# Three changes of order in an attention and mixture-of-experts kernel: loads ahead of DRAM moves, a product ahead of a turn, a routing round half a unit later

## The chip, the cores and the metric

The kernel runs on one core of a Trainium2 chip. A core has five engines that run side by side, each with its own queue of instructions: TensorE (PE in the profile, its weight loads PEld), VectorE (DVE), ScalarE (ACT), GpSimd (POOL) and SyncE (SP), which here only issues transfers (DMAs). The metric is the device time of one execution in microseconds (us), as the median of several runs.

## The reference

```python
def _attn_ref(q, k, v, S1, S2):            # q, k, v: 4 x 4 x 1088 x 32, S1, S2: 8 x 32
    def phi(x):
        a = np.einsum('rd,bhsd->bhsr', S1, x)
        b = np.einsum('rd,bhsd->bhsr', S2, x)
        return np.einsum('bhsi,bhsj->bhsij', a, b).reshape(*x.shape[:-1], r * r)
    q_p, k_p = phi(q), phi(k)
    kv = np.einsum('bhsf,bhsd->bhfd', k_p, v)
    z = np.sum(k_p, axis=2)
    num = np.einsum('bhsf,bhfd->bhsd', q_p, kv)
    den = np.einsum('bhsf,bhf->bhs', q_p, z)[..., None] + 1e-06
    return num / den

def _moe_ref(x, w_gate, w1, w2):           # x: 4352 x 128, 8 experts, w1: 128 x 1024, w2: 1024 x 128
    logits = x @ w_gate
    P = np.exp(logits - logits.max())
    for _ in range(8):
        P /= P.sum(1, keepdims=True) + 1e-09
        P /= P.sum(0, keepdims=True) + 1e-09
        P *= N / E
    for e in range(E):
        out += P[:, e:e + 1] * (np.maximum(x @ w1[e], 0.0) @ w2[e])
```

The output of the attention, with its heads side by side, is the x of the experts. Everything is float32.

## The kernel before

Attention runs batch by batch. For a batch, `keys_sums` multiplies the keys' features into the values, `times(b, c)` multiplies the two repeated halves of the queries' features for one third c of the batch in place (`ph`, times `rb`; L550 on DVE), `tops(b, c)` multiplies these features with the keys' sums on PE (L559, L563), and `over(b, c)` divides (L572 the reciprocal, L574 the quotient, L578 a turn, all on DVE). Batch b also prepares its successors: `transpose_q` turns the loaded queries of a later batch (L387 on DVE, 128x1088), and `queries_ab` projects them (L523 on PE) and sends the results through DRAM (`qa`, `qb`). All products that ACT or DVE read from PSUM, in attention and in the experts' first layer alike, take turns in four banks, `bank()`.

The experts are eight two-layer networks over 4352 rows. The rows are worked on in groups. The first groups, of experts 0 to 2, need no routing weights: they fill PE while attention and routing run. A unit of this work is a step with four matmuls of the first layer (L1183), their evacuation with the ReLU on ACT (L1187, out to `hb`), and products of the second layer (L1643). Seven products of block sums do the work of eight there; the sums of a block's activations are three instructions on DVE (L1204, one double and two single). When all seven are summed, ACT copies the four banks of sums out (L990 to L1007) and DVE adds these up at its leisure (L981, L984).

Attention and routing are generators. Each `yield` hands over a number of units, and `fill` (L1753) puts so many steps of the experts' work between the instructions before and behind the yield. `fill` also counts the steps in `passed`, and `aside` holds work that is due when a count is reached. The order on PE, DVE and ACT is the order of this program; each engine goes through its own in turn.

The later groups, of experts 1 to 7, are weighted, and their first layer needs combinations ("forms") of the blocks of W1. `forms_ahead` makes them, expert by expert, in nine pieces that `forms_at` hangs into `aside`. The first piece, `loads`, issues five transfers on SP's queue: two moves from W1 to the DRAM array `wl` (`raw_of_first`, L284) and three loads of W1's blocks into places of SBUF that attention has left (`area`; by `copied`, L304): `kx`, `ph`, `v`, `kp` and `rb`. Next, ACT turns signs (`turn`, L307), POOL issues transfers that add another block to what was turned (`plus`, L297), and SP issues transfers that write the results to `wl` and `wf` (L304). Experts 1 and 2 are due in batch 2, 3 to 7 (`forms_of_five`) in routing. The first move of expert 3 also waits for the first logits (`all_there`). The transfers on SP and on POOL are kept in the order of the program.

Routing (from L707) computes logits and then eight rounds. A round sums the rows of the routing matrix (L734), takes the reciprocal (L735), waits 1.25 units, scales (L738), sums the columns of each partition (L741, `cs`), waits 3 units, sums over the partitions by two matmuls with ones (L745, the bank `pc`), takes the reciprocal (L748) and scales (L751). The last round's result is turned (L755) and written to DRAM (`pT`), from where the weighted groups load it.

Of the kernel before, what the change touches and what calls it, by code (L numbers as in the profile page):

```python
# [43 lines left out]
def kernel(  # L44
# [24 lines left out]
    ITERS = 8  # L69
# [206 lines left out]
    def split(t):  # L276

        return t.rearrange("p (k b f) -> p k b f", k=2, b=2)

    def raw_of_first(e):  # L280

        w = fast[e][0]
        for out, x in ((w[upper], moe_w1[e][upper]), (split(w)[lower, :, 0], split(moe_w1[e])[lower, :, 0])):
            ins = tc.keep_in_program_order(nc.sync.dma_start(out=out, in_=x))  # L284
            if all_there:
                tc.add_manual_dep(ins.ins, all_there.pop(), SYNC, reason="behind the last x")

    def forms_ahead(e, area):

        w = split(moe_w1[e])  # L290
        fast[e] = [dram.tile([P, F], F32, name=f"{n}{e}") for n in ("wl", "wf")]
        wl, wf = (split(t) for t in fast[e])
        d, t3, z = (x.rearrange("p (k f) -> p k f", k=2) for x in area)
        t3 = t3[lower]

        def plus(out, x):
            tc.keep_in_program_order(nc.gpsimd.dma_start(out=out, in_=x, accum_op=Alu.add))  # L297

        def copied(queue, out, x):
            if queue in last_moves:  # L300
                with tc.issue_after(last_moves.pop(queue).ins):
                    queue.dma_start(out=out, in_=x)
            else:
                tc.keep_in_program_order(queue.dma_start(out=out, in_=x))  # L304

        def turn(out, x):
            nc.scalar.activation(out=out, in_=x, func=Act.Copy, scale=-1.0)  # L307

        def loads():
            raw_of_first(e)  # L310
            copied(nc.sync, d, w[:, :, 0])
            copied(nc.sync, t3, w[lower, :, 1])
            copied(nc.sync, z[lower], w[upper, :, 1])

        def turn_all():
            turn(area[0], area[0])
            plus(area[0], w[:, :, 1])

        def turn_low():
            turn(area[1][lower], area[1][lower])  # L320
            plus(t3, w[upper, :, 1])

        def turn_lowest():
            turn(area[2][lower], area[2][lower])

        def turn_across():
            turn(area[2][upper], area[0][lower])

        def keep_low():
            copied(nc.sync, wf[lower, :, 0], d[lower])  # L330

        def last_sum():
            plus(area[0], area[2])

        def keep_two():
            copied(nc.sync, wl[lower, :, 1], t3)
            copied(nc.sync, wf[upper, :, 0], z[upper])

        def keep_rest():
            copied(nc.sync, wf[:, :, 1], d)  # L340

        return loads, turn_all, turn_low, turn_lowest, turn_across, keep_low, last_sum, keep_two, keep_rest
# [42 lines left out]
    def transpose_q(b, lo=0, hi=S):  # L385
        to = kT if b == 1 else qT
        nc.vector.transpose(out=to[:, lo:hi], in_=loaded["q", b].rearrange("p a d -> p (a d)")[:, lo:hi])  # L387
# [55 lines left out]
    def keys_kept(b):  # L443
        pv = sums_of.pop(b)
        for s in range(2):
            sl = slice(64 * s, 64 * (s + 1))
            if b:
                x, y = kvs[b % 2][sl, :, s, :], pv[sl].rearrange("p i c d -> p i (c d)")[:, :, 0:D + 1]
            else:
                x, y = kvz[sl, :, :, s, :], pv[sl].rearrange("p i c d -> p c i d")  # L450
            nc.scalar.copy(x, y)
# [93 lines left out]
    def third(t, c):  # L545
        return t.rearrange("p i (s c n) -> p i s c n", s=2, c=3)[:, :, :, c]

    def times(b, c):
        ph = third(phs[b % 2], c)
        nc.vector.tensor_tensor(ph, ph, third(rb, c), op=Alu.mult)  # L550
# [87 lines left out]
    def attention(b):  # L638


        follows = b + 1 < B
        apart = 1.4 if follows else 1.05
        keys_sums(b)
        times(b, 0)
        yield 3.6 if b == 1 else 2
        keys_kept(b)
        times(b, 1)
        tops(b, 0)
        if b == 1:
            transpose_q(2)  # L650
        yield apart
        times(b, 2)
        over(b, 0)
        tops(b, 1)
        if b == 1:
            queries_ab(2)
            repeat_a(2)
        if follows:
            repeat_b(b + 1)
        yield apart  # L660
        over(b, 1)
        if b + 1 == B:
            take_over(b, 0, 192, nc.gpsimd)
        yield apart
        tops(b, 2)
        if follows:
            transpose_k(b + 1)
        if b + 2 < B:
            load_k(b + 2)
            load_v(b + 2)  # L670
        yield apart
        over(b, 2)
        if b + 1 < B:
            take_over(b, 0, W9, nc.gpsimd)
            if b + 2 == B:
                forms_of_two()
        else:
            take_over(b, 192, W9, nc.sync)
        if follows:
            yield 0.7  # L680
            keys_ab(b + 1)
            yield 0.7
            if b == 1:
                transpose_q(3)
            keys_products(b + 1, 0)
            yield 1.4
            keys_products(b + 1, 1)
            if b == 1:
                queries_ab(3)
                repeat_a(3)  # L690
            yield 1.4
            keys_products(b + 1, 2)
            yield 1.4
# [11 lines left out]
    def routing():  # L705

        forms_of_five()  # L707
        yield 6
        logits(0)
        logits(1)  # L710
        yield 0.5
        logits_turned()
        logits(2)
        yield 0.5
        logits_turned()
        logits_turned()
        lg = lgp[:, :, 0:E]
        mx = sk.tile([P, 1], F32, tag="mx", name="mx")
        nc.vector.tensor_reduce(out=mx, in_=lg, axis=AX.XY, op=Alu.max)
        yield 2.25  # L720
        pm = bank()[:, 0:P]
        for s in range(2):
            nc.tensor.matmul(pm[64 * s:64 * (s + 1)], mx.to_broadcast([P, 64]), ident, start=True, stop=True,
                             tile_position=(0, 64 * s))
        nc.vector.reduce_max(mx, pm, axis=AX.X)
        nc.vector.tensor_scalar(mx, mx, -1.0, 64 * math.log(2.0), op0=Alu.mult, op1=Alu.add)
        pw = p2s[0]
        nc.scalar.activation(out=pw[:, :, 0:E], in_=lg, func=Act.Exp, bias=mx[:, 0:1])

        step = 1.5 * 2.0 ** (23 - 149 + 64)  # L730
        nc.vector.tensor_scalar(pw[:, :, 0:E], pw[:, :, 0:E], step, step, op0=Alu.add, op1=Alu.subtract)
        for it in range(ITERS):
            rs = sk.tile([P, SA], F32, tag="rs", name="rs")
            nc.vector.reduce_sum(rs, pw, axis=AX.X)  # L734
            nc.vector.reciprocal(rs, rs)  # L735
            yield 1.25
            p1 = p1s[it % 2]
            nc.vector.scalar_tensor_tensor(p1[:, 0:SA], rs.unsqueeze(2).to_broadcast([P, SA, E]), UP,  # L738
                                           pw[:, :, 0:E], op0=Alu.mult, op1=Alu.mult)
            cs = sk.tile([P, E], F32, tag="cs", name="cs")  # L740
            nc.vector.reduce_sum(cs, p1.rearrange("p g e -> p e g"), axis=AX.X)  # L741
            yield 3
            pc = bank()[:, 0:E]
            for s in range(2):
                nc.tensor.matmul(pc[64 * s:64 * (s + 1)], ones[:, 0:64], cs, start=True, stop=True,  # L745
                                 tile_position=(0, 64 * s))
            cr = sk.tile([P, E], F32, tag="cr", name="cr")
            nc.vector.reciprocal(cr, pc)  # L748
            last = it == ITERS - 1
            pw = lgp if last else p2s[(it + 1) % 2]  # L750
            nc.vector.scalar_tensor_tensor(pw[:, :, 0:E], cr.unsqueeze(1).to_broadcast([P, SA, E]),  # L751
                                           float(N) / E * (1.0 if last else UP), p1[:, 0:SA],
                                           op0=Alu.mult, op1=Alu.mult)

        nc.vector.transpose(out=lgT.rearrange("p a s -> p (a s)"), in_=lgp.rearrange("p a e -> p (a e)"))  # L755
        for b in (1, 0, 2, 3):
            tc.keep_in_program_order((nc.gpsimd if b != 1 else nc.sync).dma_start(
                out=pT[:, b * S:(b + 1) * S], in_=lgT[32 * b:32 * b + E].rearrange("p a s -> p (a s)")))
# [1106 lines left out]
```

## Time and profile before

| | |
|---|---|
| time, median of 3 runs | 879.25 us |
| lowest, highest run | 878.93, 882.19 us |
| the profiled execution: its own time | 879.82 us |
| its span, first to last instruction | 878.0 us |
| granted TensorE clock, mean | 1.000 |
| matmuls | 11846, mean times 376 to 517 ns in the experts |
| transfers | 174.64 MB, mean 199 GB/s |

The time of an engine is the sum of its instructions; weight loads (PEld) run beside matmuls. Matmuls overlap: one may start before the one ahead has ended, and their ends are modelled, so the distance from one start to the next is the better measure of PE. A row of the timeline shows the start, the time, the engine, the line, what is written and read, how many instructions of one kind are merged, and in brackets the idle time before them and what ended it. One matmul instruction of the program is two in the profile. A trailing q stands for the engine's sequencer; a row of SPq is the issue of a transfer, not its run. A row of the list of transfers ends with the time from issue to landing.

### The profile page before, as it was taken

To read this page: it belongs to the slowest core of one execution; us is meant where nothing else is said; L and a number is where in the kernel's file an instruction comes from. 1 tells how busy PE (TensorE), PEld (TensorE's weight loads), DVE (VectorE), ACT (ScalarE), POOL (GpSimd) and SP (SyncE) were. 2 spreads that over 40 slices of the span, in tenths; PEclk is the share of its full clock that TensorE was granted. 3 is DMA by queue.
4 is the path that set the end of the run, shared out by engine and by line. 5 is a ranking of instruction groups with operands and counts; after the bars stand their busy time and mean duration, and the time that the engine had idled before them with its cause. 6 is when DMAs were issued, how large, how long until landed. Compare 5 with 4: busy or idle time off the path is not lost.

```text
span 878.0 us, 28825 instructions
## 1 busy us (share of the span) xinstructions
PE 871.7 (99%) x11846; PEld 638.4 (73%) x11846; DVE 790.2 (90%) x1631; ACT 570.4 (65%) x1309; POOL 176.8 (20%) x246
## 2 busy tenths in 40 slices
PE   9999999999999999999999999999999999999998
PEld 6687544566778888887878787878787777766665
DVE  8679688889999999999999999999998999998975
ACT  3455678668676767676666666766766666765653
POOL 2221332121122212221132112221221122200000
PEclk9999999999999999999999999999999999999999
DMA  9998699576778787777786776687577776774430
GB/s 256 284 286 298 135 249 221 136 171 208 219 208 238 214 257 210 199 211 210 209 210 188 210 207 181 184 244 215 159 179 229 217 209 184 204 206 97 119 81 13
DMA packets 97459, 174.64 MB, mean 199 GB/s; under 512 B 29088, under 2 KB 68848, under 8 KB 92480
## 3 DMA queue, kind: packets, MB, share of 16 engines
q1 hardware_dynamic: 74904, 139.65, 50.0%
q0 software_dynamic: 21264, 33.00, 21.9%
q8 instruction: 93, 1.52, 0.7%
q10 hardware_dynamic: 1160, 0.15, 0.1%
q14 instruction: 38, 0.31, 0.1%
HBM read 125.67 MB, written 25.08 MB: 172 GB/s over the span
## 4 chain that ended last, share of the span: by engine, by line
PE 95%; DVE 3%; DMA 1%; issue 0%; DVEq 0%
PE s L1643 42%; PE a L1351 38%; PE a L1183 12%; DMA qx<-in_q_dram 1%; PE a L436 1%; DVE hb L1204 1%; PE a L559 1%; PE a L404 0%; PE s L465 0%; PE a L523 0%; DMA raw<-in_S_dram 0%; PE a L600 0%; PE a L485 0%; PE s L485 0%; DVE rs L734 0%
## 5 line engine op out<-in xcount | busy, mean ns | idle before, releaser
L1351 PE MATMUL a<-xe,w 64*64 64x384 f32 x2164 | 417.3, 483 | 0.0
L1643 PE MATMUL s<-hb,ws 64*64 64x256 f32 (+4 forms) x2980 | 383.2, 383 | 0.0
L1643 PE MATMUL s<-hx,ws 64*64 64x256 f32 (+1 forms) x2908 | 349.4, 376 | 0.0
L1351 PE MATMUL a<-de,w 64*64 64x384 f32 x1600 | 304.6, 483 | 0.0
L1643 PEld LDWEIGHTS s<-hb,ws 64*64 64x64 f32 (+1 forms) x2980 | 205.6, 133 | 65.7 <-issue 17.6
L1643 PEld LDWEIGHTS s<-hx,ws 64*64 64x64 f32 (+1 forms) x2908 | 198.1, 133 | 55.3 <-issue 8.2
L1253 DVE TENSOR_TENSOR hb<-hb 128x512 f32<-128x512 f32 (+1 forms) x340 | 187.8, 577 | 1.3 <-ACT hb L1386 1.1
L1351 PEld LDWEIGHTS a<-xe,w 64*64 64x64 f32 x2164 | 144.5, 133 | 16.3 <-DVE a L1391 1.3
L1386 ACT ACTIVATE hx<-a 128x384 f32<-128x384 f32 x204 | 96.8, 492 | 59.4 <-PE a L1351 57.6
L1386 ACT ACTIVATE hb<-a 128x384 f32<-128x384 f32 x204 | 97.3, 492 | 57.6 <-PE a L1351 56.8
L1183 PE MATMUL a<-xT,w 128*64 128x256 f32 (+3 forms) x576 | 128.2, 453 | 0.0
L1351 PEld LDWEIGHTS a<-de,w 64*64 64x64 f32 x1600 | 110.7, 133 | 19.4 <-ACT hb L1386 0.8
L1253 DVE TENSOR_TENSOR hx<-hx 128x512 f32<-128x512 f32 (+1 forms) x204 | 118.3, 595 | 0.0
L909 POOL DMA_DIRECT2D de<-xe x68 | 57.2, 991 | 299.8 <-PE a L1351 157.9
L1187 ACT ACTIVATE hb<-a 128x256 f32<-128x256 f32 (+3 forms) x150 | 67.7, 453 | 55.3 <-PE a L1183 50.4
L1382 ACT ACTIVATE hb<-a 128x384 f32<-128x384 f32 x136 | 66.7, 491 | 34.1 <-PE a L1351 33.0
L1380 ACT COPY a<-a 128x384 f32<-128x384 f32 x136 | 63.0, 464 | 34.8 <-PE a L1351 34.3
L1391 DVE TENSOR_TENSOR a<-a,hb 128x384 f32<-128x384 f32 x136 | 76.7, 564 | 9.7 <-PE a L1351 8.5
L1183 PEld LDWEIGHTS a<-xT,w 128*64 128x64 f32 x576 | 53.9, 137 | 29.7 <-issue 10.4
L1204 DVE TENSOR_TENSOR hb<-hb 128x416 f32<-128x416 f32 (+7 forms) x90 | 59.8, 664 | 16.2 <-ACT hb L1187 11.2
L1643 PE MATMUL s<-hb,w 128*64 128x256 f32 (+4 forms) x296 | 70.4, 431 | 0.0
L909 POOL DMA_DIRECT2D de<-de x34 | 29.6, 872 | 124.4 <-issue 63.5
(235 smaller groups left out, 1014.2 us busy)
## 6 DMA issues: line engine op xcount, KB each, us to landing
ws<-ws SPq DMA_DIRECT2D x34, 1280.0 KB, 6.5
w<-wl SPq DMA_DIRECT2D x34, 512.0 KB, 7.7
w<-wf SPq DMA_DIRECT2D x33, 512.0 KB, 8.8
px<-pT SPq DMA_DIRECT2D x34, 384.0 KB, 9.5
w<-in_moe_w_dram SPq DMA_DIRECT2D x15, 512.0 KB, 4.7
de<-xe POOLq DMA_DIRECT2D x34, 192.0 KB, 3.3
de<-de POOLq DMA_DIRECT2D x34, 192.0 KB, 8.2
ws<-in_moe_w_dram SPq DMA_DIRECT2D x7, 512.0 KB, 8.3
```

Source lines behind the costliest of these rows:

```text
L436: nc.tensor.matmul(pv[64 * s:64 * (s + 1), i], kp[:, H * t + h].rearrange("p i j -> p (i j)"), vx[:, slots[h], t, :], start=(t == 0 and i ...
L909: tc.keep_in_program_order(nc.gpsimd.dma_start(out=out, in_=x, accum_op=Alu.add))
L1183: nc.tensor.matmul(ph[sl], loaded_w[j][0][:, P * f + H2 * s:P * f + H2 * (s + 1)], sources[j][:, lo:hi], start=True, stop=True, tile_posit ...
L1187: last_relu[:] = [nc.scalar.activation(out=out, in_=ph, func=Act.Relu).ins.name]
L1204: nc.vector.tensor_tensor(out, a, b, op=Alu.subtract)
L1253: nc.vector.tensor_tensor(places(out), places(a), places(b), op=Alu.subtract if off else Alu.add)
L1351: nc.tensor.matmul(out[sl], w[r, c0 + H2 * s:c0 + H2 * (s + 1)], x[r], start=start, stop=stop, tile_position=(H2 * row, H2 * s), skip_grou ...
L1380: witness(k, p, 1, nc.scalar.copy(b, bx))
L1382: witness(k, p, 5, nc.scalar.activation(out=m5s[p], in_=b, func=Act.Copy, scale=1.0 if p else -1.0))
L1386: ins = nc.scalar.activation(out=out, in_=x, func=Act.Relu)
L1391: ins = nc.vector.tensor_tensor(by if what == 1 else raw(k, p, 1, 1), bb[p], m5s[p], op=Alu.add)
L1643: mm = nc.tensor.matmul(sums[g][i][H2 * s:H2 * (s + 1), n * place:n * (place + 1)], w, x, start=c == (2 if halves and row is None else 1) ...
```

## The change

Three orders are changed; no instruction is added or removed.

```diff
@@ forms_ahead @@
         def loads():
-            raw_of_first(e)
+            if e <= 3:
+                raw_of_first(e)
             copied(nc.sync, d, w[:, :, 0])
             copied(nc.sync, t3, w[lower, :, 1])
             copied(nc.sync, z[lower], w[upper, :, 1])
+            if e > 3:
+                raw_of_first(e)
@@ attention @@
         times(b, 1)
         tops(b, 0)
         if b == 1:
+            times(b, 2)
             transpose_q(2)
         yield apart
-        times(b, 2)
+        if b != 1:
+            times(b, 2)
         over(b, 0)
@@ routing @@
             nc.vector.reduce_sum(cs, p1.rearrange("p g e -> p e g"), axis=AX.X)
-            yield 3
+            yield 3.5 if it == ITERS - 2 else 3
             pc = bank()[:, 0:E]
```

For experts 4 to 7 the three loads are issued ahead of the two moves. In batch 1 the third product on `ph` stands ahead of the turn of batch 2's queries, not behind it. In the seventh of the eight rounds of routing, 3.5 units lie between the columns' sums and the matmuls with ones. On PE these matmuls so come one step later: behind two more instructions L1183 and two more L1643. On DVE the two single sums L1204 of a block and one sum L981 come ahead of that round's reciprocal L748, L751, and the next round's L734 and L735. ACT's and POOL's orders stay the same.

## The prediction

> **What bounds the kernel now.** I read the page first: busy time by engine and the chain that ended last.
>
> ```profile
> span 878.0 us, 28825 instructions
> PE 871.7 (99%) x11846; PEld 638.4 (73%) x11846; DVE 790.2 (90%) x1631; ACT 570.4 (65%) x1309; POOL 176.8 (20%) x246
> ...
> PE 95%; DVE 3%; DMA 1%; issue 0%; DVEq 0%
> ```
>
> TensorE (PE) has work for 871.7 of 878.0 us and carries 95% of the chain. A re-ordering can only win what PE loses in gaps, so the next view is the list of PE's waits. Two of its rows name lines that the diff touches.
>
> ```profile
> PE a L745 <- DVE cs L741: 0.4, 1, 0.4
> PE a L523 <- DVE rd L574: 0.3, 1, 0.3
> ```
>
> These figures are too small, because the ends of matmuls are modelled and overlap the next start. The real loss is the distance between two starts less the usual distance, and I read it below from the timelines. The third edit touches no line in this list; there I looked at what ScalarE (ACT) and VectorE (DVE) wait for around the turns of the forms.
>
> **Part by part.** The changed program has the same DMAs and the same arithmetic instructions. Only places in queues move: one DVE product, one pair of PE matmuls with the DVE normalization behind it, and eight moves on SP's queue.
>
> *Batch 1's third ph product (L550) ahead of the turn of batch 2's queries (L387).*
>
> ```profile
> 32.35 1.83 DVE L550 TENSOR_TENSOR ph<-ph,rb 128x768 f32<-128x768 f32 x2 [5.41 <-DMA rb<-qb]
> 35.99 1.31 DVE L387 STREAM_TRANSPOSE qT<-qx 128x1088 f32<-128x1088 f32 x1 [1.82 <-DMA qx<-in_q_dram]
> 37.23 0.92 DVE L550 TENSOR_TENSOR ph<-ph,rb 128x768 f32<-128x768 f32 x1
> ...
> 38.32 0.56 DVE L574 TENSOR_TENSOR rd<-a,rc 128x384 f32<-128x384 f32 x1
> ```
>
> ```profile
> 34.81 0.24 PE L563 MATMUL a<-eps,ones 128*64 128x12 f32 x4
> 34.90 0.69 PE L1183 MATMUL a<-xT,w 128*64 128x288 f32 x4
> ...
> 38.38 0.24 PE L563 MATMUL a<-eps,ones 128*64 128x12 f32 x4
> 38.93 1.20 PE L523 MATMUL a<-qT,wdq 128*64 128x192 f32 x12 [0.31 <-DVE rd L574]
> ```
>
> DVE stands idle for 1.82 us until the queries have landed, turns them, and only then makes the product, whose operands were there all the time. The quotient L574 comes behind it, ends at 38.32 + 0.56 = 38.88, and PE's L523 starts at 38.93. After L563, PE's next start usually follows after 34.90 - 34.81 = 0.09 us; here it took 38.93 - 38.38 = 0.55, so 0.46 us are lost. In the changed order the product (0.92) lies inside the idle 1.82 and ends at about 35.1. The turn still starts at 35.99, and L574 ends 0.92 - 0.08 (the two overlap so much: 35.99 + 1.31 against 37.23) = 0.84 earlier, at 38.04, ahead of the 38.47 at which PE is free. Gain: the whole 0.46 us. If the queries landed before 35.1, the product would delay the turn, but then all of it would also be earlier; I see no loss.
>
> *Experts 4 to 7: arrays ahead of the moves of W1.* The case that shows is expert 5, whose arrays lie in rb.
>
> ```profile
> 118.63 1.82 SPq L284 DMA_DIRECT2D wl<-in_moe_w_dram  x2
> 120.49 2.87 SPq L304 DMA_DIRECT2D rb<-in_moe_w_dram  x3
> ```
>
> ```profile
> wl<-in_moe_w_dram SPq DMA_DIRECT2D x1, 256.0 KB, 6.3
> ...
> rb<-in_moe_w_dram SPq DMA_DIRECT2D x1, 256.0 KB, 7.5
> ```
>
> ```profile
> 125.26 0.52 ACT L1187 ACTIVATE hb<-a 128x416 f32<-128x416 f32 x1 [0.23 <-PE a L1183]
> 128.05 0.63 ACT L307 ACTIVATE rb<-rb 128x512 f32<-128x512 f32 x1 [2.27 <-DMA rb<-in_moe_w_dram]
> ...
> 130.03 0.50 ACT L990 COPY z<-s 64x416 f32<-64x416 f32 x1
> ...
> 134.21 0.52 ACT L1187 ACTIVATE hb<-a 128x416 f32<-128x416 f32 x1
> ```
>
> SP's queue is strictly in order: two moves from DRAM to DRAM, then three loads. The first load was issued at 120.49, landed 7.5 us later at 128.0, and ACT, which had ended at 125.78, held everything behind its turn L307 until 128.05. With the loads first, that load is issued at 118.63. If it takes the landing of the move of equal size it replaces (6.3 us), it is there at 124.9 and the wait is gone; with its own 7.5 us it is there at 126.1 and 0.35 remains. So ACT runs on 1.9 to 2.3 us earlier. The moves come about 2.9 us later, and what they write is read only by the loads of the weighted experts' stage, behind all of routing.
>
> What of it reaches PE? Behind the turn, ACT was late with evacuating PE's banks (L1187), and through it the sums on DVE and then PE:
>
> ```profile
> 134.76 1.03 DVE L1204 TENSOR_TENSOR hb<-hb 128x832 f32<-128x832 f32 x1 [1.45 <-ACT hb L1187]
> ```
>
> ```profile
> 136.36 0.20 PEld L1183 LDWEIGHTS a<-xT,w 128*64 128x64 f32 x4 [0.52 <-ACT hb L1187]
> ...
> 138.53 0.13 PEld L1643 LDWEIGHTS s<-hb,ws 128*64 128x64 f32 x1 [0.58 <-DVE hb L1204]
> ...
> 139.98 0.14 PEld L1643 LDWEIGHTS s<-hb,w 128*64 128x64 f32 x2 [0.21 <-issue]
> 140.76 0.23 PEld L745 LDWEIGHTS a<-cs,ones 128*64 128x64 f32 x4 [0.64 <-ACT hb L1187]
> ```
>
> The weight loads usually stand 0.21 us apart; three gaps of 0.52, 0.58 and 0.64 hold 1.74 - 3 x 0.21 = 1.11 us too much. That is the upper bound of the gain. The lower one is nothing: at 130.03 ACT starts seven copies of finished sums (L990 on), which PE must have finished first, and whatever lead ACT has by then can be lost there. I take 0.4, nearer to nothing, since seven copies at 0.50 fill most of the time from 130.03 to the evacuation at 134.21, whatever ACT's lead was. DVE's late start at 134.76 then moves by about as much.
>
> [...]
>
> *Routing's seventh round half a unit later.* On PE the pair L745 of round seven moves behind one more step (L1183 twice, L1643 twice in the program). On DVE a pair of sums (L1204) and one leisurely sum (L981) move ahead of the reciprocal L748 and the three instructions behind it.
>
> ```profile
> 159.15 0.49 PE L1643 MATMUL s<-hb,w 128*64 128x384 f32 x1
> ...
> 159.47 0.49 PE L1643 MATMUL s<-hb,w 128*64 128x384 f32 x1
> ...
> 160.45 0.29 PE L745 MATMUL a<-cs,ones 128*64 128x8 f32 x4 [0.44 <-DVE cs L741]
> ```
>
> ```profile
> 159.65 0.66 DVE L741 TENSOR_REDUCE cs<-p 128x8 f32<-128x280 f32 x1
> 160.22 0.58 DVE L981 TENSOR_TENSOR kept<-z,f 128x416 f32<-128x416 f32 x1
> 160.72 0.95 DVE L1204 TENSOR_TENSOR hb<-hb 128x768 f32<-128x768 f32 x1
> 161.59 0.20 DVE L748 RECIPROCAL cr<-a 128x8 f32<-128x8 f32 x1
> ...
> 163.09 1.09 DVE L1204 TENSOR_TENSOR hb<-hb 128x384 f32<-128x384 f32 x2
> 164.21 0.59 DVE L981 TENSOR_TENSOR kept<-z,m 64x416 f32<-64x416 f32 x1
> ...
> 165.31 0.67 DVE L741 TENSOR_REDUCE cs<-p 128x8 f32<-128x280 f32 x1
> ...
> 168.64 0.21 DVE L748 RECIPROCAL cr<-a 128x8 f32<-128x8 f32 x1 [0.61 <-PE a L745]
> ```
>
> ```profile
> 167.37 0.14 PEld L745 LDWEIGHTS a<-cs,ones 128*64 128x64 f32 x1
> ```
>
> Two starts usually lie 159.47 - 159.15 = 0.32 us apart. PE should have gone on at 159.79 and went on at 160.45, 0.14 after the column sums cs ended (159.65 + 0.66 = 160.31): 0.66 us lost. One step is eight halves of 0.32 in two column tiles, about 1.3 us. So PE would want cs at 159.79 + 1.3 = 161.1 at the present pace, and at 160.2 when the two other edits have brought it 0.86 forward. DVE has cs at 160.31, less the 0.4 of the second edit: 159.9. The wait is gone: gain 0.66.
>
> What is late next? On DVE 1.09 + 0.59 = 1.68 us go ahead of L748, so round seven ends 1.68 later; but L738 and L741 of round eight stood behind the same instructions anyway, so its cs keeps 165.31 + 0.67 = 165.98. PE's L745 of round eight loads its weights at 167.37, which leaves 1.39 us, plus DVE's 0.4, less the 0.14: PE may come 1.65 us earlier before it waits there.
>
> *The sum:* 0.46 + 0.4 + 0.66 = 1.52, just inside 1.65. The profiled execution took 879.82 (span 878.0): 878.3. Its fellows' median is 879.25, 0.57 below it; the same 1.5 off that gives **877.8**.
>
> **The rivals.**
> - *The load lands no sooner.* POOL's transfers are in flight at the same time, and if these set the landing, ACT waits on. For it: 7.5 us for 256 KB says that the queues are full. Against it: the equal move ahead of it took only 6.3. Then 0.46 + 0.66 = 1.12: 878.1.
> - *Given back in round eight, or slower: DVE blocks on the sums put ahead of round seven's reciprocal.* They would start at 160.72 + 0.95 = 161.67.
>
> ```profile
> 161.55 0.49 ACT L1187 ACTIVATE hb<-a 128x384 f32<-128x384 f32 x1 [1.64 <-PE a L1183]
> 162.83 0.49 ACT L1187 ACTIVATE hb<-a 128x384 f32<-128x384 f32 x1 [0.79 <-DVE rs L734]
> ```
>
> Given back: if they need the evacuation that ends at 162.83 + 0.49 = 163.32, DVE stands for 1.65 us, which uses up the 1.65 of room, and PE waits in round eight until it has its old time again: 879.2. Slower: if they need the one after that, 162.83 - 161.55 = 1.28 later, DVE stands for 2.93, and round eight comes 2.93 - 1.65 = 1.28 later than it did: 880.5. From 1.65 us of standing on, the loss is real. Against it: the first sum of the block (0.95 at 160.72) reads all four evacuations in the code, so the pair behind it should find them there. [...]
>
> **How the numbers follow.** Forecast 0.55, load no sooner 0.22, given back 0.12, slower 0.08, something else 0.03. Low end: 0.46 + 1.11 + 0.66 = 2.23 gives 877.0, and the three runs lie some tenths apart (878.93 and 879.25), so 876.7. High end: past the given-back case to 880.1, which leaves out most of the slower one. About 0.5%, 4.4 us, is what a measurement of this kernel tells from no change; every case above lies inside it. So within 0.5%: 0.92; faster 0.03; slower 0.05, for a collision that I do not see.
>
> **What would show it.** In the profile after: no row for L523 and none for the seventh round's column matmul among PE's waits; L550 three times in a row before the turn, and the turn's idle below 1 us; ACT's 2.27 us wait for rb gone or below 0.4; the three gaps in the weight loads at 136 to 141 smaller by a third or more; round eight's column matmul without a wait. The prediction is wrong if a new wait of over 0.5 us stands at that matmul or at the seventh round's L1204, or if the arrays of rb still land 7 us or more after 118.6 + 1.

## The result and the profile after

| | before | after |
|---|---|---|
| median of 22 runs | 879.29 us | 878.46 us |
| lowest, highest run | 878.42, 882.19 us | 877.63, 879.61 us |
| ratio of the times, after to before | | 0.9986, 95% interval 0.9979 to 0.9992 |
| the profiled execution: its own time | 879.82 us | 878.69 us |
| its span | 878.0 us | 876.9 us |

The kernel became 0.83 us faster by the medians, and 0.0014 x 879.29 = 1.2 us (0.7 to 1.8) by the ratio. Forecast were 1.5 us and 877.8 us. The change is real, since the interval lies below 1, and smaller than the 0.5% that the forecast took as the bound of no change; an interval 0.13% wide shows that this bound was too wide.

The page of after, with the span, the busy times and the chain that ended last:

```profile
span 876.9 us, 28825 instructions
...
PE 871.3 (99%) x11846; PEld 640.5 (73%) x11846; DVE 790.3 (90%) x1631; ACT 570.2 (65%) x1309; POOL 176.7 (20%) x246
...
PE 99%; DMA 1%; SPq 0%; DVE 0%; issue 0%; DVEq 0%
```

TensorE's work is as long as before (871.3 against 871.7 us), so what went were gaps. Its part of the chain rises from 95 to 99%, but this is no measure of the change: the unchanged kernel, profiled again below, has 98%. The list of PE's waits is whole here; its columns are the total, the number and the longest, in us.

```profile
PE a L107 <- POOL own L109: 1.0, 1, 1.0
PE s L468 <- DVE qT L390: 0.3, 1, 0.3
```

The two rows at which the change aimed, L745 and L523 (now L750 and L526: lines behind the edits move by 3 to 5), are gone. The row of L468 is new; it lies in the first 9 us, in code that the change doesn't touch.

*The product.* DVE's and then PE's timeline of after around batch 1's products:

```profile
34.09 2.69 DVE L553 TENSOR_TENSOR ph<-ph,rb 128x768 f32<-128x768 f32 x3 [6.25 <-DMA rb<-qb]
36.70 1.30 DVE L390 STREAM_TRANSPOSE qT<-qx 128x1088 f32<-128x1088 f32 x1
...
38.15 0.56 DVE L577 TENSOR_TENSOR rd<-a,rc 128x384 f32<-128x384 f32 x1
```

```profile
35.87 0.27 PE L566 MATMUL a<-eps,ones 128*64 128x12 f32 x4
...
39.44 0.27 PE L566 MATMUL a<-eps,ones 128*64 128x12 f32 x4
39.53 1.21 PE L526 MATMUL a<-qT,wdq 128*64 128x192 f32 x12
```

Three products stand in a row, the turn follows with no idle time, and L526 starts 0.09 us behind L566, where it took 0.55.

*The loads.* SP's issues and ACT's timeline of after (ACT's L1192 was L1187):

```profile
118.60 1.99 SPq L304 DMA_DIRECT2D rb<-in_moe_w_dram  x3
120.63 1.42 SPq L284 DMA_DIRECT2D wl<-in_moe_w_dram  x2
```

```profile
125.81 0.52 ACT L1192 ACTIVATE hb<-a 128x416 f32<-128x416 f32 x1 [0.23 <-PE a L1188]
126.23 0.62 ACT L307 ACTIVATE rb<-rb 128x512 f32<-128x512 f32 x1
...
144.21 0.49 ACT L1192 ACTIVATE hb<-a 128x384 f32<-128x384 f32 x1 [0.24 <-PE a L1188]
...
168.33 1.09 ACT L1192 ACTIVATE hb<-a 128x384 f32<-128x384 f32 x2 [0.93 <-PE a L1188]
...
815.65 0.38 ACT L1192 ACTIVATE hx<-a 128x256 f32<-128x256 f32 x1 [0.48 <-PE a L1188]
```

The loads go first, and ACT turns rb right behind the evacuation at 125.81: its wait of 2.27 us is gone. The load did not get faster: in the list of transfers it lands 7.2 us after its issue (7.5 before), so at 118.60 + 7.2 = 125.8, and ACT comes to it at 126.23. Of the forecast's two landings, 6.3 and 7.5 us behind the issue, the second was nearer. The weight loads that showed the three gaps of 0.52 to 0.64 us (in after the rows at 135.92, 138.01 and 140.10) now stand at the usual 0.2 behind the one ahead, or closer:

```profile
135.91 0.14 PEld L1648 LDWEIGHTS s<-hb,ws 128*64 128x64 f32 x1 [0.20 <-issue]
135.92 0.14 PEld L1188 LDWEIGHTS a<-xT,w 128*64 128x64 f32 x1
...
138.01 0.14 PEld L1648 LDWEIGHTS s<-hb,ws 128*64 128x64 f32 x1 [0.21 <-DVE hb L1209]
...
140.10 0.14 PEld L750 LDWEIGHTS a<-cs,ones 128*64 128x64 f32 x2 [0.21 <-issue]
```

*The rounds.* DVE's and PE's timelines of after in rounds seven and eight:

```profile
158.89 0.66 DVE L746 TENSOR_REDUCE cs<-p 128x8 f32<-128x280 f32 x1
159.47 0.58 DVE L986 TENSOR_TENSOR kept<-z,f 128x416 f32<-128x416 f32 x1
159.97 2.13 DVE L1209 TENSOR_TENSOR hb<-hb 128x768 f32<-128x768 f32 x3
...
162.73 0.21 DVE L753 RECIPROCAL cr<-a 128x8 f32<-128x8 f32 x1
...
164.84 0.66 DVE L746 TENSOR_REDUCE cs<-p 128x8 f32<-128x280 f32 x1
...
167.57 0.21 DVE L753 RECIPROCAL cr<-a 128x8 f32<-128x8 f32 x1
```

```profile
160.69 0.28 PE L750 MATMUL a<-cs,ones 128*64 128x8 f32 x4
...
166.61 0.23 PE L750 MATMUL a<-cs,ones 128*64 128x8 f32 x2
```

Round seven's column sums end at 158.89 + 0.66 = 159.55, and PE comes for them 1.14 us later. In round eight it is 166.61 - 165.50 = 1.11. Neither round has a wait, and the sums put ahead of the reciprocal (three L1209 in a row, 2.13 us) don't block.

**Where the time went.** The same instruction in two profiles gives the lag of one behind the other. The rows of before that aren't shown yet are three of ACT's evacuations:

```profile
144.61 0.49 ACT L1187 ACTIVATE hb<-a 128x384 f32<-128x384 f32 x1 [0.24 <-PE a L1183]
...
169.39 1.09 ACT L1187 ACTIVATE hb<-a 128x384 f32<-128x384 f32 x2 [0.93 <-PE a L1183]
...
816.71 0.39 ACT L1187 ACTIVATE hx<-a 128x256 f32<-128x256 f32 x1 [0.48 <-PE a L1183]
```

| place | before | after | lag of after | step |
|---|---|---|---|---|
| first L563 | 34.81 | 35.87 | +1.06 | the start +1.06 |
| projection L523 | 38.93 | 39.53 | +0.60 | product -0.46 |
| evacuation ahead of rb | 125.26 | 125.81 | +0.55 | -0.05 |
| first evacuation of 128x384 | 144.61 | 144.21 | -0.40 | loads -0.95 |
| the pair behind round eight | 169.39 | 168.33 | -1.06 | round -0.66 |
| experts | 816.71 | 815.65 | -1.06 | 0 |

The three edits win 0.46 + 0.95 + 0.66 = 2.07 us between these two executions, and nothing is given back later. But after began 1.06 us later, in the first 35 us, where TensorE runs the same code in both. Of this, 0.89 us are there at 8.67, in the row of L468 (7.78 in before); the rest comes at L562, which waits for the first product on ph, and DVE stood for rb until 34.09 (32.35 in before). Both numbers need other executions: the late start, and whether before always loses 2.07.

### The profile page after: what moved, and what is told of

The parts are those of the page before. It is cut to its first block, busy times and chain, and to the rows that moved or that the text cites. A ratio compares the mean times of both kernels' runs of the same rounds, so it can differ in the third digit from the quotient of the medians.

```text
span 876.9 us, 28825 instructions
## 1 busy us (share of the span) xinstructions
PE 871.3 (99%) x11846; PEld 640.5 (73%) x11846; DVE 790.3 (90%) x1631; ACT 570.2 (65%) x1309; POOL 176.7 (20%) x246
## 3 DMA queue, kind: packets, MB, share of 16 engines
q8 instruction: 93, 1.52, 0.7%
## 4 chain that ended last, share of the span: by engine, by line
PE 99%; DMA 1%; SPq 0%; DVE 0%; issue 0%; DVEq 0%
PE s L1648 43%; PE a L1356 38%; PE a L1188 14%; PE a L439 1%; PE a L562 1%; DMA qx<-in_q_dram 1%; PE s L468 0%; PE a L526 0%; PE a L407 0%; PE a L603 0%; PE s L488 0%; PE a L488 0%; SPq L158 0%; PE a L468 0%; SPq L95 0%; PE a L566 0%
## 5 line engine op out<-in xcount | busy, mean ns | idle before, releaser
L1192 ACT ACTIVATE hb<-a 128x256 f32<-128x256 f32 (+3 forms) x150 | 67.7, 453 | 56.0 <-PE a L1188 50.0
L1209 DVE TENSOR_TENSOR hb<-hb 128x416 f32<-128x416 f32 (+7 forms) x90 | 59.8, 664 | 15.0 <-ACT hb L1192 10.4
```

What stands on the lines that cost most here:

```text
L1192: last_relu[:] = [nc.scalar.activation(out=out, in_=ph, func=Act.Relu).ins.name]
L1209: nc.vector.tensor_tensor(out, a, b, op=Alu.subtract)
```

## The experiments

Each kernel ran against before on one chip, in turns; ratios are to before, with a 95% interval. A stretch is measured on ACT's evacuations of the table above: from the one ahead of the turn of rb to the first of 128x384 (19.35 us in before, 18.40 in after), and on to the pair behind round eight (24.78 and 24.12).

### Before once more, and each edit alone

Before again, unchanged:

> The kernel before, unchanged, as a measure of how far two executions of one program differ. In the two profiles at hand, batch 0's work before 36 us stands 1.07 us later after the change than before, though nothing there was changed. Theory A (the start varies from execution to execution): this profile's start up to 36 us differs from the first one's by some tenths to 1 us, and PE's gap ahead of L523 differs with it, from 0 to 0.5 us; the gaps at 134 to 141 us (1.1 us in the weight loads) and ahead of L745 at 160 us (0.66) are there again within 0.1. Rival B (the start is fixed, and the change itself moves it): start and all gaps as in the first profile within 0.1 us. Time: 0.0 us off, +-0.5.

The loads alone:

```diff
-            raw_of_first(e)
+            if e <= 3:
+                raw_of_first(e)
...
+            if e > 3:
+                raw_of_first(e)
```

> The first edit alone: for experts 4 to 7 the three loads ahead of the two moves. Theory A (each part takes its own gap away): ACT's wait of 2.27 us for rb is gone or below 0.4, the gaps in the weight loads at 136 to 141 us shrink from 1.1 us to 0.2, ACT stands 0.9 to 1.0 us earlier at 142 us than in the kernel before, measured from 120 us on; PE's wait ahead of L745 at 160 us stays at about 0.6, since DVE gets ahead by as much as PE. Time 0.9 us less (878.4). Rival B (a lead won there is lost at round seven, where DVE is late): the wait ahead of L745 grows to over 1.2 us and the time is 0.3 us less or the same.

The product alone:

```diff
         if b == 1:
+            times(b, 2)
             transpose_q(2)
         yield apart
-        times(b, 2)
+        if b != 1:
+            times(b, 2)
```

> The second edit alone: batch 1's third product ahead of the turn. Theory A: no wait of PE ahead of L523, ACT 0.46 us earlier at 42 us than in the kernel before, measured from 36 us on, kept to the end: 0.46 us less (878.8). Rival B (a late start already hides this wait in many executions, because the queries land at a time of their own): the wait is gone, but the mean gain is 0.2 us or less, not to be told from nothing. Rival C (a lead won at 39 us is lost where ACT waits for rb at 128 us, which is bound by transfers): ACT's wait there grows from 2.3 to 2.7 us and the time is the same.

The round alone:

```diff
-            yield 3
+            yield 3.5 if it == ITERS - 2 else 3
```

> The third edit alone: the seventh round's matmuls half a unit later. Theory A: PE's wait of 0.44 us ahead of L745 (0.66 between starts) is gone, none comes in round eight, ACT is 0.66 us earlier from 162 us on than in the kernel before, measured from 150 us: 0.66 us less (878.6). Rival B (DVE is the bound until round eight): round eight's L745 waits for cs by 0.3 us or more, and the time is 0.3 us less at most.

| kernel | median (before: 879.82) | ratio | wait for rb | to 128x384 | to round eight |
|---|---|---|---|---|---|
| before again | 879.71 us | 0.9999 [0.9990, 1.0007] | 1.25 | 18.39 | 24.71 |
| loads | 879.00 us | 0.9992 [0.9984, 1.0001] | none | 18.39 | 24.42 |
| product | 879.22 us | 0.9993 [0.9979, 1.0007] | 2.32 | 19.40 | 24.77 |
| round | 878.63 us | 0.9994 [0.9985, 1.0003] | 1.35 in two waits | 18.53 | 24.12 |

By their times no edit alone can be told from nothing: each interval holds 1. The traces tell more. ACT's timeline of before again:

```profile
125.07 0.52 ACT L1187 ACTIVATE hb<-a 128x416 f32<-128x416 f32 x1 [0.23 <-PE a L1183]
126.83 0.63 ACT L307 ACTIVATE rb<-rb 128x512 f32<-128x512 f32 x1 [1.25 <-DMA rb<-in_moe_w_dram]
...
143.46 0.49 ACT L1187 ACTIVATE hb<-a 128x384 f32<-128x384 f32 x1 [0.24 <-PE a L1183]
```

The same kernel waited 2.27 us for rb in one execution and 1.25 in another: the load, issued at about the same time (120.49 and 120.29), took 7.5 us to land and then 6.5. With 1.25 the stretch is as short as with the loads ahead (18.39), so up to the first evacuation of 128x384 the first 1.3 us of that wait cost nothing. They are not free altogether: the next stretch is 24.71 in before again and 24.42 with the loads ahead, since DVE is late at round seven (there PE loses 0.57 us between starts against 0.30). That the gaps behind the wait would come again within 0.1 us was expected, and did not happen. Nor does the gap at L523 come back in before again:

```profile
34.54 1.31 DVE L387 STREAM_TRANSPOSE qT<-qx 128x1088 f32<-128x1088 f32 x1
35.77 0.92 DVE L550 TENSOR_TENSOR ph<-ph,rb 128x768 f32<-128x768 f32 x1
```

```profile
38.38 0.24 PE L563 MATMUL a<-eps,ones 128*64 128x12 f32 x4
38.47 1.18 PE L523 MATMUL a<-qT,wdq 128*64 128x192 f32 x12
```

The queries had landed in time, DVE turned them 1.45 us earlier than in the first profile, and PE went on after 0.09 us. Of six profiles with the old order of the product and the load of batch 2's queries in its place (before, before again, loads, round, and two further down) one has the gap, the one on which the forecast was built.

The wait at round seven's column matmul is of another kind: it is there in both profiles of before (0.4 in the list of waits), and with the round alone the second stretch is 24.12 in place of 24.78 and 24.71. With the loads alone it was expected to stay at 0.6 us; there it was 0.30, of which more below.

### All three again, the load's delay doubled, later queries

The whole change again:

> All three edits, unchanged. The four profiles of the last look show that the gap ahead of L523 and the wait for rb change from execution to execution: with the old order the first stood at 0.5 us in one profile of three and the second at 2.3, 1.2, 1.3 and 2.3 us in four. Theory (the first two edits take away what some executions lose, the third what all lose): no PE wait ahead of L523, no ACT wait for rb over 0.4 us, no PE wait in rounds seven and eight; the step in ACT's lateness from 124 to 170 us is within 0.1 us of the first profile's of the change (1.6 us less than the kernel before in its first profile). Time 0.8 to 1.2 us below the kernel before. Rival (the waits only move): one of these three waits is there with over 0.5 us.

From before, expert 6's two moves are put ahead of expert 5's arrays too, so that four moves stand ahead of the loads of rb and none ahead of expert 6's ("the ring's order" of the expectation is this order on SP's queue):

```diff
-            raw_of_first(e)
+            for i in {5: (5, 6), 6: ()}.get(e, (e,)):
+                raw_of_first(i)
```

> From the kernel before: expert 5's loads stand behind four moves, its own two and those of expert 6, which are taken from ahead of expert 6's loads. The opposite of the first edit, once more. Theory A (the ring's order sets the landing): the load of rb is issued 1.5 to 2 us later and lands as much later; ACT's wait for rb is 3 to 4.5 us, PE's gaps behind it (128 to 142 us) grow from 0.1 to 1.0 in the kernel before to 2 to 3 us; 1.5 us more time (881). Rival B (the total traffic of all queues sets it): ACT waits as before, 1.2 to 2.3 us, time within 0.5 us.

Batch 2's queries load behind its keys, in before (the old order) and in after (the new one):

```diff
         divide(0, 2)
-        load_q(2)
...
         load_k(2)
+        load_q(2)
```

> From the kernel before: batch 2's queries are loaded behind its keys, not ahead, so they land some 2 us later than 36.0 in the first profile. With the old order of product and turn. Theory (the turn's wait for the queries is what makes PE wait ahead of L523): PE's wait there grows to 2 us or more, time 1 to 2 us more, less what other gaps take up. Rival (the wait ahead of L523 has another cause): no more than 0.5 us there.

> All three edits and batch 2's queries loaded behind its keys. Theory: PE waits ahead of L523, 0.84 us less than in the old order with late queries, since the product (0.92) is done by then; the rest of the profile as after the change. Rival: PE waits as long as with the old order, since the projection itself needs the turned queries; then the second edit has worth only for a wait of under 0.5 us.

| kernel | median (before: 879.47) | ratio | wait for rb | to 128x384 | to round eight |
|---|---|---|---|---|---|
| all again | 878.60 us | 0.9990 [0.9981, 0.9999] | none | 17.80 | 24.12 |
| double | 882.78 us | 1.0045 [1.0027, 1.0063] | 4.73 | 21.80 | 24.77 |
| late queries, old order | 879.60 us | 0.9999 [0.9990, 1.0008] | 1.6 in two waits | 18.88 | 24.77 |
| late queries, new order | 879.34 us | 0.9996 [0.9986, 1.0005] | none | 18.39 | 24.12 |

In all again the first stretch is 0.6 us shorter only because it begins late: ahead of the evacuation at 127.15 ACT stood 0.82 us for another array of the forms, in the turn `kp<-ph` at 126.50. From the evacuation before that, at 125.16, it takes 19.79 us to 144.95, as in after (124.42 to 144.21). So with the loads ahead a wait for an array can still occur, and this one cost TensorE nothing.

SP's issues and ACT's timeline with the moves doubled:

```profile
118.89 4.23 SPq L284 DMA_DIRECT2D wl<-in_moe_w_dram  x4
123.17 1.99 SPq L304 DMA_DIRECT2D rb<-in_moe_w_dram  x3
```

```profile
125.31 0.52 ACT L1188 ACTIVATE hb<-a 128x416 f32<-128x416 f32 x1 [0.23 <-PE a L1184]
130.55 0.63 ACT L307 ACTIVATE rb<-rb 128x512 f32<-128x512 f32 x1 [4.73 <-DMA rb<-in_moe_w_dram]
```

The loads are issued 123.17 - 120.49 = 2.7 us later than in the profile of before, behind four moves whose issue takes SP 4.23 us (two: 1.82), ACT waits 4.73 - 2.27 = 2.46 longer, and the stretch is 21.80 - 19.35 = 2.45 longer: past the first 1.3 us the whole wait reached TensorE here. The wait should cost 4.73 - 1.3 = 3.4 us, and before itself loses 0.5 on average (see below), so 2.9 are to be expected between the medians. Measured are 882.78 - 879.47 = 3.3 from four runs, 2.4 to 5.5 by the interval, and twice the 1.5 us that had been expected.

The landing follows the issue. From issue to landing the load of rb takes 6.8 us on average in the five profiles with the two moves ahead of it (6.2 to 7.5) and 6.7 in the seven with them behind it (6.0 to 7.6), and here its turn starts 130.55 - 123.17 = 7.4 behind the issue. So the rival that the load lands no sooner falls. What makes it 6.0 us in one execution and 7.6 in another, POOL's transfers perhaps, stays open.

Late queries were meant to make the product's gap sure. In the old order they didn't: of the twelve matmuls that the profile has for the projection only the last four waited (0.35 us, not the 2 us expected). These have a bank of their own, so the two banks were probably given out the other way round; no view shows the bank. What the pair does show is DVE's part. The rows of the old order, then of the new:

```profile
36.88 1.31 DVE L387 STREAM_TRANSPOSE qT<-qx 128x1088 f32<-128x1088 f32 x1 [2.33 <-DMA qx<-in_q_dram]
38.12 0.92 DVE L550 TENSOR_TENSOR ph<-ph,rb 128x768 f32<-128x768 f32 x1
...
39.21 0.56 DVE L574 TENSOR_TENSOR rd<-a,rc 128x384 f32<-128x384 f32 x1
```

```profile
38.00 1.31 DVE L390 STREAM_TRANSPOSE qT<-qx 128x1088 f32<-128x1088 f32 x1 [1.92 <-DMA qx<-in_q_dram]
...
39.46 0.56 DVE L577 TENSOR_TENSOR rd<-a,rc 128x384 f32<-128x384 f32 x1
```

From the turn's start to the quotient's end it takes 39.77 - 36.88 = 2.89 us in the old order and 40.02 - 38.00 = 2.02 in the new: the product is worth 0.87 behind the turn (forecast: 0.84). On PE the pair went against the expectation: in the new order, where the queries landed 1.12 us later than in the old, PE waits longer (0.87 us at L526, ahead of all twelve). So the new order takes away a short wait, not every one.

### Pairs, and a wider step

Loads and product without the round, loads and round without the product, and all three with a seventh round that yields more:

> The first two edits without the third. With the first edit DVE is forward as well as PE: in its profile alone PE went on 0.29 us late at round seven's L745, against 0.66 and 0.57 in the two profiles of the kernel before. Theory: the same here, 0.25 to 0.35 us between starts, no ACT wait for rb, no PE wait ahead of L523; time 0.3 us above the kernel with all three, 0.6 below the kernel before. Rival (the 0.29 was chance, the third edit is worth 0.6 in any case): the wait at L745 is 0.55 us or more.

> The first and the third edit without the second. In the profiles with the old order of product and turn, PE waited ahead of L523 in one of five, where the queries landed late (36.0 us). Theory: no wait there in most executions, 0.5 us in a few; everything else as with all three; time as with all three within 0.3 us. Rival (the second edit has a steady worth of 0.46): PE waits ahead of L523 and the time is 0.4 us or more above that of all three.

```diff
-            yield 3.5 if it == ITERS - 2 else 3
+            yield 4.5 if it == ITERS - 2 else 3
```

> All three edits, but the seventh round 1.5 units later instead of 0.5. Theory (round eight's margin sets how far the round can be moved): the work of another step, about 2.2 us on DVE, goes ahead of round seven's reciprocal, cs of round eight comes about as much later than in the changed kernel, and PE, which had 0.9 us there, waits 1 us or more at round eight's L745 (L750 in this kernel); time 0.5 to 1.5 us above all three. Rival (DVE has room enough): no wait there, same time.

| kernel | median (before: 879.64) | ratio | wait for rb | to 128x384 | to round eight |
|---|---|---|---|---|---|
| loads and product | 879.01 us | 0.9993 [0.9981, 1.0005] | none | 18.39 | 24.44 |
| loads and round | 878.61 us | 0.9986 [0.9976, 0.9995] | none | 18.39 | 24.12 |
| all, 4.5 units | 878.40 us | 0.9983 [0.9974, 0.9993] | none | 18.39 | 24.01 |

Leaving the product out costs nothing that shows: 878.61 is as good as the 878.46 and 878.60 of the whole change. Leaving the round out costs 24.44 - 24.12 = 0.32 us of the second stretch. That is less than the 0.66 of the round alone, and the loads alone already make it 24.42, 0.36 less than in before. The reason can be read from after: from the evacuation ahead of rb (lag +0.55) to the end of round seven's column sums (159.55 against 160.31, lag -0.76) DVE comes forward by 1.31 us, PE by 0.95. So DVE brings 0.36 of the wait back by itself, and the loads and the round overlap.

The wider step missed its expectation. The units are owed on from yield to yield, and the eighth round's column matmuls also came one step later. The block that the forecast's slower rival feared then appeared one round on, in DVE's timeline:

```profile
167.93 0.96 DVE L1209 TENSOR_TENSOR hb<-hb 128x768 f32<-128x768 f32 x1 [1.47 <-ACT hb L1192]
168.81 0.20 DVE L753 RECIPROCAL cr<-a 128x8 f32<-128x8 f32 x1
```

DVE stood 1.47 us for an evacuation, ahead of the last reciprocal, and ACT later stood 1.3 us for the routing's result from DRAM. PE waited for neither, and the time is no worse: there is room behind round eight as well. That the stretch is 0.11 shorter need not be a gain: round eight's column matmuls, which in after lie inside it, come behind its end here (168.39 against 167.41). 878.40 doesn't beat 878.46 by anything that these intervals can tell.

## Why the prediction was right, and what its terms were worth

The forecast case happened: each step did what was predicted of it, and the sum has the right sign and about the right size (0.8 to 1.2 of 1.5 us). Its terms were off in both directions.

- **The product, 0.46.** Right in the execution profiled, and for the reason given (0.55 became 0.09; 0.87 us won on DVE for 0.84). Mis-sized as a mean: the gap needs queries that land late, and one of six profiles had it. 0.46 / 6 is 0.08 us.
- **The loads, 0.4 (0 to 1.11).** In the execution profiled it was 0.95, near the upper bound. What failed is the choice of the lower end, "seven copies ... fill most of the time": they took at most 0.16 of the 1.11. What is free, as far as this stretch goes, is the first 1.3 us of the wait (before again), and behind it all counts (double). As a mean it is less: the five profiles with the loads behind one expert's moves lost 0.96, 0.00, 1.01, 0.14 and 0.49 against 18.39, 0.5 on average. Two errors, one in each direction, came out near 0.4, and that was luck.
- **The round, 0.66.** Right alone (24.78 to 24.12, and 24.71 in before again). Beside the loads 0.3 of it is left. The step that failed is that DVE has cs only 0.4 earlier while PE comes 0.86 earlier, so that the whole 0.66 remained to be won: DVE came forward by more than PE (1.31 against 0.95 behind the loads).
- **Room in round eight, 1.65 less 1.52 = 0.13 left.** In fact 1.11 were left. Against their lag of 1.06 at the start, DVE's cs of round eight came 165.98 - 165.50 + 1.06 = 1.54 forward and PE's matmul 167.69 - 166.61 + 1.06 = 2.14; the forecast had 0.4 and 1.52. DVE was 1.82 forward at round seven already (0.51 up to the evacuation ahead of rb, 1.31 behind it) and lost 0.28 of it until round eight. The forecast also counted the room from the weight load at 167.37, and the matmul itself started at 167.69 in before.
- **The correction by 0.57 to the median** was taken as chance. The runs show its parts: the profiled execution of before had the second longest wait for rb of five and the only gap at L523, and an early start. Before again started as early (34.81), other kernels later by up to 1.8 us: all again has that L566 at 36.60 and after at 35.87. The traces name two places: PE's first waits for turned keys and queries as these land (L468's 0.3 us in after, 0.7 in all again), and L562, which needs the product that waits for rb from DRAM (in all again DVE stands for rb until 34.82, that product ends at 35.77, and PE goes on at 35.88 after 0.85 us; the evacuation that its list of waits names had ended at 35.12). Why these landings differ is open.

With means in place of one execution's values the sum is 0.1 + 0.5 + 0.66, less up to 0.36 of overlap where the wait for rb was long: 0.9 to 1.3 us. Measured: 0.83 by medians, 1.2 (0.7 to 1.8) by the ratio, and 0.9 (0.1 to 1.7) by the ratio of all again.

The rivals: "the load lands no sooner" fell, as none of the seven profiles with the loads ahead has a wait at rb, though the closest (loads and round) escapes it by 0.2 us: issued at 119.22, landed 7.1 later, turned at 126.50. ACT's shorter waits for kp near 120 us (0.20 to 1.09 in all six profiles with the moves ahead) are gone in these seven too. "Given back" and "slower" fell: three sums of 768 in a row took 2.13 us without idle time, as argued from the first sum of that block, and the lag of -1.06 stays the same from round eight to the experts. That DVE can block there is real (1.47 us with the wider step), but not at the place and the price forecast.

The load's time from issue to landing is 6.8 us on average in the five profiles with the two moves ahead of it and 6.7 in the seven with them behind it, so what moved the landing is the time of the issue. The forecast read full queues from the 7.5 us. What the traces show is a mean busy share of the 16 DMA engines of 1.03 from 118 to 128 us in before, where the load took 7.5 us, and of 1.08 in after, where it took 7.2.

## What to carry to other kernels

A stall in one profile is a sample: profile the unchanged kernel twice before pricing it, and count only what is there both times. A wait on an engine off the path can have a free part, which two executions with different waits show (here, up to the next landmark, 1.25 us cost nothing and 2.27 cost 0.96); what lay past it was paid in full here (2.46 us more of the wait made the stretch 2.45 us longer). Look one stage further too: the free part made another engine late, and some 0.3 us were paid there. Do not add the gains of two edits that bring the same operand forward: measure the later wait with the earlier edit in place.

## What had not been expected

- The landing of one load varies between executions of the same program: ACT's wait for rb was 2.27 and 1.25 us in two profiles of before, while the evacuation ahead of the wait stood at 125.26 and 125.07. Over twelve profiles the same load took 6.0 to 7.6 us from issue to landing.
- The first 35 us differ by up to 1.8 us between executions in which TensorE has the same instructions up to there (34.81 against 36.60), as much as the whole change was forecast to win.
